# Batch 0 of an attention and MLP kernel: k and q of three head pairs loaded as bf16 by GpSimd's queue, fills moved to VectorE, and the front in another order

## The chip, the cores and the metric

The kernel runs on one core of one Trainium2 chip. The core has five engines, each with its own instruction queue: TensorE (PE in the profile, with its weight loads as PEld), VectorE (DVE), ScalarE (ACT), GpSimd (POOL) and SyncE (SP). The metric is the time of one execution on the device, in microseconds; lower is better.

## The reference

Four batches of chunked attention with 8 memory rows, and behind it an MLP with a snake activation. Cut to what matters:

```python
B, H, S, D = 4, 8, 768, 64;  chunk, left_ctx, right_ctx = 32, 16, 8;  n_mem = 8
for c in range(S // chunk):                       # 24 chunks
    q_c    = q[:, :, 32*c : 32*c + 32]
    k_full = concat(mem_k, k[:, :, max(0, 32*c - 16) : min(S, 32*c + 40)])
    v_full = concat(mem_v, v[:, :, same rows])
    a      = softmax(q_c @ k_full.T / 8)
    out[:, :, 32*c : 32*c + 32] = a @ v_full
x = out.transpose(0, 2, 1, 3).reshape(3072, 512)
h = x @ w_in                                      # 512 -> 2048
g = h + sin(alpha * h)**2 / (alpha + 1e-9)
result = g @ w_out                                # 2048 -> 512, float32
```

## The kernel before

Matmuls run in bf16 with sums in f32. A batch has 768 rows; its attention gives xT (features on the partitions, rows along them), and a dense stage per batch computes h = xT times w_in in 16 tiles of 128 features (`half_tile`, L458, 4 matmuls for each half of the rows), the sine on ACT (L473), the square (`squared`), the sum into gT on VectorE (L485) and the matmul with w_out (L496). The attention of batch b + 1 runs inside the dense stage of batch b. Only batch 0 has nothing to hide in: its attention is the *front*, `Stage(-1)`, and the dense stage of batch 0 begins when its xT is there.

The order of all work is written out by hand, as strings of words; each word calls one method of `Stage`, and every engine takes its instructions in the order in which the words issue them. Words that matter here, for head pair 0 to 3:

- `k0`, `l0`: `turn`, which transposes k or q of a pair on PE into a PSUM bank (L279 for batch 0, L285 for the other batches); `K0A`, `L0V`: `put_k` and `put_q`, which copy the result into kT and qT (L296 and L310) on ACT (A) or VectorE (V). `put_k` also copies the two ends, always on VectorE (L302).
- `a0A`, `a4V`: the cast of k (0 to 3) or q (4 to 7) of a pair from f32 to bf16 (L689).
- `s01`: scores of pair 0, half 1: the mask (L328), eight score matmuls (L336) and one exponential on ACT into pt (L343). `n0`: row sums by matmuls with ones (L358). `y0`, `r0`: on ACT, the logarithm of the sums (L367) and the exponential of its negative (L372), which gives 1/sum. `v01`: values of a pair and half (L378) and their product with 1/sum into xT (L383, VectorE).
- `z1`: one matmul of 512 columns on a tile of zeros into a bank that is not in use (L723); nothing reads its result.
- `V002`: loads v of heads 0 and 1 of batch 0; `I02`, `U69`: load column blocks of w_in and row blocks of w_out; `dq108`: loads q of batch 1, all heads, as bf16 (`load_one`, L155). All of these are DMAs of GpSimd's queue, which can convert f32 to bf16 on the way. `m0` copies the memory values into the v tile (L188).
- `Cb`, `Ci` and so on: constants. `Cb` and `Cm` make the score mask, `Ci` a table of it for `mind` (L799 to L805), `Cf` an f32 identity (L822), `Ck` the transposed memory keys (L811), `Cw` the bf16 memory values (L825), `Cl` alpha, `Cz`, `Cv`, `Cp` and `Cs` fill the borders of kT, the ones beside v, the ends of pt and the borders of kst.

k and q of batch 0 are loaded as f32 by SyncE's queue, eight loads of two heads each, and cast on chip. In the f32 tile the two heads lie one after the other; the cast interleaves them (`beside`), so that one transpose of 128 columns turns both heads at once: six per pair. The other batches load bf16 straight, and `turn` then needs one transpose per head: twelve of 64 columns.

Of the kernel before, what the change touches and what calls it, by code (L numbers as in the profile page):

```python
# [9 lines left out]
P = 128  # L10
# [5 lines left out]
F32 = mybir.dt.float32  # L16
ACTF = mybir.ActivationFunctionType
ALU = mybir.AluOpType
# [67 lines left out]
def kernel(  # L86
# [12 lines left out]
    nc = tc.nc  # L99
    B, H, S, D = q.shape  # L100
# [3 lines left out]
    NJ = S // QW  # L104
    HP = H // 2
# [9 lines left out]
    mlp = ctx.enter_context(tc.tile_pool(name="mlp", bufs=4))  # L115
# [7 lines left out]
    ident = consts.tile([P, P], BF, name="ident")  # L123
# [3 lines left out]
    asum = consts.tile([P, 8], BF, name="asum")  # L127
    mind = consts.tile([P, NJ, 3, 32], BF, name="mind")
# [12 lines left out]
    q_bf = consts.tile([P, H, 6, D], BF, name="q_bf")  # L141
# [124 lines left out]

    def beside(src, hp):

        return src[:, 2 * hp:2 * hp + 2].rearrange("p h r d -> p (h r d)").rearrange(
            "p (r h d) -> p r h d", r=6, h=2)

    def turn(b, src, hp):
        bank, bs = banks.single()
        t = bank[:, 0:384].bitcast(BF).rearrange("p (r c) -> p r c", r=6)
        if b == 0:
            for r in range(6):
                nc.tensor.transpose(  # L279
                    t[:, r, :], beside(src, hp)[:, r].rearrange("p h d -> p (h d)"), ident[:]  # L280
                )
            return t, bs
        for r in range(6):
            for e in range(2):
                nc.tensor.transpose(  # L285
                    t[64 * e:64 * e + 64, r, :], src[:, 2 * hp + e, r, :], ident[:]
                )
        return t, bs
# [248 lines left out]
    class Stage:  # L537
# [81 lines left out]
        def do_k(self, a):  # L619
            self.piece["k" + a] = turn(self.b, k_bf, int(a))  # L620

        def do_l(self, a):
            self.piece["q" + a] = turn(self.b, q_bf, int(a))
# [62 lines left out]
        def do_a(self, a):  # L686
            hp = int(a[0]) % HP
            dst = kq[int(a[0]) // HP]
            copier(a[1])(  # L689
                beside(dst, hp).rearrange("p r h d -> p h r d"),  # L690
                kq_f[int(a[0])][:].rearrange("p h (r d) -> p h r d", d=D),
            )
# [44 lines left out]

    kq_f = [mlp.tile([P, 2, 6 * D], F32, name="kq_f", tag=t) for t in ("u", "s2") * 4]  # L740
    memk_f = mlp.tile([P, H, D], F32, name="memk_f", tag="o_sb", bufs=3)
    alpha_rows = mlp.tile([FT, P], F32, name="alpha_rows", tag="o_sb", bufs=3)
    memv_f = mlp.tile([P, H, D], F32, name="memv_f", tag="o_sb", bufs=3)
# [1 line left out]
    def load_f(src, hp, t):  # L745
        nc.sync.dma_start(
            t[:], src[0, 2 * hp:2 * hp + 2].rearrange("h (p r) d -> p h (r d)", p=P)
        )

    nc.vector.memset(zeros[:], 0.0)  # L750
    nc.vector.memset(tiny[:], 0.0)
    load_f(k, 0, kq_f[0])
    load_f(q, 0, kq_f[4])
    for bb in range(B):
        if not CROSSED[bb][0]:
            nc.scalar.dma_start(memk_f[NM * bb:NM * bb + NM], mem_k[bb].rearrange("h n d -> n h d"))
    nc.scalar.dma_start(memv_f[64:72], mem_v[0].rearrange("h n d -> n h d"))
    nc.scalar.preload_act_table_set("natural_log_exp_and_others")
    for hp in (1, 2, 3):
        load_f(k, hp, kq_f[hp])  # L760
        load_f(q, hp, kq_f[4 + hp])
    nc.sync.dma_start(alpha_rows[:], moe_alpha.rearrange("(ft p) -> ft p", p=P))
    nc.vector.memset(ones[:], 1.0)
    nc.vector.memset(mcol[:], 0.0)
    masks.make_identity(nc, ident[:])
    for vw in vws:
        nc.gpsimd.memset(vw[0:32, 0, 0, 0:D], 0.0)
        nc.gpsimd.memset(vw[96:128, H - 1, NJ - 1, 0:D], 0.0)

    rows = ((0, 0, 56), (1, 32, 96), (2, 64, 128), (3, 16, 56), (4, 64, 120), (5, 64, 72))  # L770

# [23 lines left out]
        nc.vector.tensor_copy(mrow[:], mt)  # L795
        banks.give(bs)

    def const_i():
        nc.gpsimd.tensor_tensor(out=asum[:, 0:5], in0=ident[:, 0:5], in1=ident[:, 64:69], op=ALU.add)  # L799
        nc.gpsimd.tensor_tensor(out=asum[:, 5:7], in0=asum[:, 0:3:2], in1=asum[:, 3:5], op=ALU.add)  # L800
        nc.gpsimd.tensor_copy(
            mind[:], asum[:, 0:3].unsqueeze(1).unsqueeze(3).to_broadcast([P, NJ, 3, 32])
        )
        nc.gpsimd.tensor_copy(mind[:, 0, 0, :], asum[:, 5:6].to_broadcast([P, 32]))
        nc.gpsimd.tensor_copy(mind[:, NJ - 1, 2, :], asum[:, 6:7].to_broadcast([P, 32]))  # L805

    def const_k():
        bank, bs = banks.single()
# [23 lines left out]
        nc.vector.reciprocal(inv_alpha[:], alpha_sb[:])  # L832
        banks.give(bs)

    def const_z():
        for kT in kTs:
            nc.gpsimd.memset(kT[:, :, 0:16], 0.0)
            nc.gpsimd.memset(kT[:, :, 848:856], 0.0)

    def const_p():  # L840
        for pt in pts:
# [6 lines left out]
    def const_s():  # L848
        nc.gpsimd.memset(kst[0:32, 0, :], 0.0)
        nc.gpsimd.memset(kst[96:128, NJ - 1, :], 0.0)  # L850

    consts_of = dict(b=const_b, m=const_m, i=const_i, k=const_k, l=const_l, p=const_p, v=const_v,
                     s=const_s, z=const_z, f=const_f, w=const_w)

    first = {}
    stage = Stage(-1, None)
    stage.tile = first
    stage.run((
# [4 lines left out]
    ))  # L863
    for i, words in enumerate(((
# [54 lines left out]
```

## Time and profile before

| | us |
|---|---|
| median of 3 runs | 215.26 (214.52 to 215.56) |
| the profiled execution | 213.6 |
| its span, first to last instruction | 211.8 |
| busy in the span: PE, PEld | 201.2, 111.8 |
| busy in the span: DVE, ACT, POOL | 139.4, 144.8, 100.2 |
| dense matmuls of batch 0 unbroken from | 23.38 |

Times in the rows count from the start of the span. An engine's busy time is the union of its instructions; a matmul's row is longer than its share of PE, since matmuls are pipelined. A row of the time order has the start, the duration, the engine, the line of the kernel, the operation and the tiles; "x6" says that six equal instructions in a row are merged; what stands in brackets is the idle time of the engine ahead of it and what ended it. The chain of waits is followed back from the last instruction to whatever released each one. The landing of a load is when its semaphore tells that all data is there.

### The profile page before, as it was taken

How to read it: one execution, taken by the hardware profiler on the slowest of the kernel's cores; microseconds unless marked ns; L12 is line 12 of the kernel's file. 1: busy time of each engine (PE TensorE's matmuls, PEld its weight loads, DVE VectorE, ACT ScalarE, POOL GpSimd, SP SyncE). 2: the span in 40 equal slices, each digit the busy share in tenths (PEclk: the TensorE clock that was granted, in tenths of full speed). 3: DMA queues.
4: the chain of work that ended last, by engine and by line, in shares of the span. 5: the costliest groups of instructions: out<-in, count | busy, mean ns of one | idle time of the engine just before them, and what ended most of it. 6: DMA issues, size and time to landing. Idle time of an engine off the chain costs nothing.

```text
span 211.8 us, 4339 instructions
## 1 busy us (share of the span) xinstructions
PE 201.2 (95%) x1654; PEld 111.8 (53%) x1654; DVE 139.4 (66%) x211; ACT 144.8 (68%) x229; POOL 100.2 (47%) x140
## 2 busy tenths in 40 slices
PE   2978999999999999999999999999999999999993
PEld 1545565655455555554456555554555455554442
DVE  5896698998453669958585569895446287864011
ACT  4789898958837579969817398968764299991110
POOL 8997609496596490029981068589200022200000
DMA  6999999999999899949999339959744400000312
GB/s 204 321 195 161 208 207 204 205 156 176 180 158 106 163 145 130 165 99 112 142 224 128 102 57 150 181 87 143 150 117 108 136 0 3 0 2 14 137 50 99
DMA packets 95852, 28.20 MB, mean 133 GB/s; under 512 B 84808, under 2 KB 92376, under 8 KB 95832
## 3 DMA queue, kind: packets, MB, share of 16 engines
q0 software_dynamic: 68608, 13.25, 87.5%
q1 hardware_dynamic: 27008, 14.63, 27.9%
q8 instruction: 13, 0.21, 0.5%
q14 instruction: 7, 0.06, 0.1%
q10 hardware_dynamic: 216, 0.05, 0.1%
HBM read 29.66 MB, written 6.29 MB: 170 GB/s over the span
## 4 chain that ended last, share of the span: by engine, by line
PE 75%; DVE 12%; DMA 4%; issue 3%; ACT 3%; SPq 1%; POOL 1%; DVEq 0%
PE ps L496 35%; PE ps L458 32%; DMA kq_f<-in_k_dram 3%; PE ps L448 3%; DVE gT L485 2%; PE ps L419 2%; DVE s L481 2%; DVE qT L310 2%; DVE kT L296 2%; ACT u L473 1%; ACT s L478 1%; DMA xT<-x_blk 1%; DVE k_bf L689 1%; PE ps L405 1%; POOL s L481 1%
## 5 line engine op out<-in xcount | busy, mean ns | idle before, releaser
L496 PE MATMUL ps<-w_out_sb,gT 128*128 128x512 bf16 (+2 forms) x400 | 89.1, 371 | 0.0
L458 PE MATMUL ps<-xT,w_in_sb 128*128 128x384 bf16 x512 | 86.2, 326 | 1.1 <-DVE gT L485 0.4
L485 DVE SCALAR_TENSOR_TENSOR gT<-s,inv_alpha,ps 128x768 bf16<-128x768 f32 x64 | 63.1, 1012 | 12.3 <-ACT s L478 5.3
L458 PEld LDWEIGHTS <-w_in_sb 128*128 128x128 bf16 x512 | 49.7, 98 | 36.2 <-issue 3.0
L473 ACT ACTIVATE u<-ps,alpha_sb 128x768 f32<-128x768 f32 x64 | 56.6, 895 | 17.5 <-PE ps L458 15.0
L496 PEld LDWEIGHTS <-gT 128*128 128x128 bf16 x400 | 36.5, 98 | 37.9 <-DVE gT L485 0.2
L481 POOL TENSOR_TENSOR s<-u 128x768 f32<-128x768 f32 x11 | 17.2, 1568 | 67.1 <-ACT u L473 66.9
L433 ACT ACTIVATE pt<-ps,biasm 128x256 bf16<-128x256 f32 x72 | 27.2, 490 | 10.5 <-PE ps L419 10.5
L503 DVE COPY o_sb<-ps 128x512 f32<-128x512 f32 (+1 forms) x15 | 10.1, 678 | 28.3 <-PE ps L496 26.4
L481 DVE TENSOR_TENSOR s<-u 128x768 f32<-128x768 f32 x23 | 21.9, 953 | 7.8 <-ACT u L473 7.7
L478 ACT ACTIVATE s<-u 128x768 f32<-128x768 f32 x30 | 25.0, 841 | 0.5
L503 ACT COPY o_sb<-ps 128x512 f32<-128x512 f32 (+1 forms) x10 | 5.6, 562 | 21.6 <-PE ps L496 21.6
L393 DVE TENSOR_TENSOR x_blk<-ps,rinv 96x512 bf16<-96x512 f32 x24 | 16.5, 686 | 0.8
L179 POOL DMA_DIRECT2D vw<-in_v_dram x13 | 13.8, 1061 | 0.6 <-issue 0.6
L172 POOL DMA_DIRECT2D vw<-in_v_dram x13 | 11.8, 906 | 4.9 <-PE ps L405 4.9
L238 POOL DMA_DIRECT2D kst<-in_k_dram x16 | 12.7, 794 | 2.0 <-DMA vw<-in_v_dram 1.3
L392 DVE RECIPROCAL rinv<-ps 96x8 f32<-96x8 f32 x24 | 4.8, 198 | 12.5 <-PE ps L448 11.3
L232 POOL DMA_DIRECT2D kst<-in_k_dram x16 | 10.9, 682 | 3.4 <-DMA vw<-in_v_dram 2.8
L245 POOL DMA_DIRECT2D q_bf<-in_q_dram x12 | 10.7, 911 | 0.0
L448 PEld LDWEIGHTS <-pt 128*128 128x128 bf16 x192 | 8.2, 97 | 4.2 <-ACT pt L433 0.3
L448 PE MATMUL ps<-vw,pt 128*128 128x65 bf16 x192 | 8.9, 193 | 0.0
L408 ACT COPY xT<-ps 128x384 bf16<-128x384 bf16 x6 | 3.1, 509 | 7.7 <-PE ps L405 7.7
(91 smaller groups left out, 139.2 us busy)
## 6 DMA issues: line engine op xcount, KB each, us to landing
out_dram<-o_sb SPq DMA_DIRECT2D x23, 256.0 KB, 2.3
kq_f<-in_k_dram SPq DMA_DIRECT2D x4, 384.0 KB, 6.0
kq_f<-in_q_dram SPq DMA_DIRECT2D x4, 384.0 KB, 5.8
q_bf<-in_q_dram POOLq DMA_DIRECT2D x12, 128.0 KB, 6.5
w_in_sb<-in_moe_w_in_dram POOLq DMA_DIRECT2D x1, 1152.0 KB, 13.3
vw<-in_v_dram POOLq DMA_DIRECT2D x8, 112.0 KB, 7.5
vw<-in_v_dram POOLq DMA_DIRECT2D x7, 128.0 KB, 7.4
kst<-in_k_dram POOLq DMA_DIRECT2D x14, 64.0 KB, 4.8
```

The costliest lines, as they stand in the source:

```text
L179: nc.gpsimd.dma_start(vw[72:128, c0:hi, 0:D], win(vflat, base + QW * c0 + 48, hi - c0, 56))
L238: nc.gpsimd.dma_start(kst[72:72 + n, j, :].rearrange("p (h d) -> p h d", d=D), k[b, :, QW * j + 48:QW * j + 48 + n, :].rearrange("h p d -> ...
L393: nc.vector.tensor_tensor(out=x_blk[:].rearrange("p g e d -> p e g d"), in0=otv[0:QW, :, :, 0:D], in1=rinv[:].unsqueeze(3).to_broadcast([Q ...
L433: nc.scalar.activation(pt[:, 0:H * QW].rearrange("p (g e c) -> p g e c", g=2, e=4)[:, :, :, 32 * m:32 * m + 32], sc[:, :, 0:4 * QW].rearra ...
L448: nc.tensor.matmul(otv[:, e, hp, :], pt[:, QW * i:QW * i + P], vws[b % 2][:, 2 * hp + e, j, 0:D + 1],)
L458: nc.tensor.matmul(t["hT"][:, hf, 0:HALF], w_in_sb[:, kt, P * t["ft"]:P * t["ft"] + P], t["xT"][:, kt, HALF * hf:HALF * hf + HALF], start= ...
L473: nc.scalar.activation(t["u"][:], t["hT"][:, :, 0:HALF], ACTF.Sin, scale=alpha_sb[:, ft:ft + 1])
L478: nc.scalar.activation(s2[:], u[:], ACTF.Square)
L481: e.tensor_tensor(out=s2[:], in0=u[:], in1=u[:], op=ALU.mult)
L485: nc.vector.scalar_tensor_tensor(out=gT[:, ft, :].rearrange("p (e c) -> p e c", e=2), in0=t["s2"][:], scalar=inv_alpha[:, ft:ft + 1], in1= ...
L496: nc.tensor.matmul(o[:, c0:c1], gT[:, ft, P * s:P * s + P], w_out_sb[:, ft, c0:c1], start=(ft == 0), stop=(ft == FT - 1),)
L503: copier(state["engines"][state["o"] % len(state["engines"])])(o_sb[:, c0:c1], o[:, c0:c1])
```

## The change

Only pair 0 of batch 0 keeps the f32 load, the cast and the six whole transposes (`HARD`). k and q of pairs 1 to 3 are loaded as bf16 by GpSimd's queue (`dk024` and its like: k, batch 0, heads 2 to 3) and turned head by head, twelve transposes, as in the other batches; their six casts go. The fills of ident, of the v borders (L767, L768), of the kT borders and the table of `Ci` move from GpSimd to VectorE; the f32 identity moves from ACT to VectorE, the cast of the memory values from VectorE to ACT. The order of the front is written anew: 21 zero matmuls where there were 8, and `Cs`, which fills kst for batch 2, comes last.

```diff
+    HARD = ((0, False), (0, True))
...
     def turn(b, src, hp):
...
-        if b == 0:
+        if b == 0 and (hp, src is q_bf) in HARD:
             for r in range(6):
...
-    kq_f = [mlp.tile([P, 2, 6 * D], F32, name="kq_f", tag=t) for t in ("u", "s2") * 4]
+    kq_f = [None] * 8
+    for hp, isq in HARD:
+        kq_f[hp + HP * isq] = mlp.tile([P, 2, 6 * D], F32, name="kq_f", tag="u" if isq else "s2")
...
+    nc.vector.memset(ident[:], 0.0)
     nc.vector.memset(zeros[:], 0.0)
     nc.vector.memset(tiny[:], 0.0)
-    load_f(k, 0, kq_f[0])
-    load_f(q, 0, kq_f[4])
+    for hp, isq in HARD:
+        load_f(q if isq else k, hp, kq_f[hp + HP * isq])
...
-    for hp in (1, 2, 3):
-        load_f(k, hp, kq_f[hp])
-        load_f(q, hp, kq_f[4 + hp])
...
-    masks.make_identity(nc, ident[:])
+    masks.make_identity(nc, ident[:], nomemset=True)
     for vw in vws:
-        nc.gpsimd.memset(vw[0:32, 0, 0, 0:D], 0.0)
-        nc.gpsimd.memset(vw[96:128, H - 1, NJ - 1, 0:D], 0.0)
+        nc.vector.memset(vw[0:32, 0, 0, 0:D], 0.0)
+        nc.vector.memset(vw[96:128, H - 1, NJ - 1, 0:D], 0.0)
...
-    def const_i():
+    def const_i(eng="P"):
+        e = nc.gpsimd if eng == "P" else nc.vector
...
-    def const_z():
+    def const_z(eng="P"):
+        e = nc.gpsimd if eng == "P" else nc.vector
...
-        'Cb z1 Cz CfA Ci a0A V002 Ck Cs Cm k0 a4V K0A a1V V024 CwV Cp z1 l0 z1 L0A m0 a5A s01 k1 '
+        'z1 z1 Cb z1 dk024 CfV z1 dq024 CiV z1 CwA z1 dk046 dk068 Ck Cv Cm dq046 a4V z1 z1 a0A z1 '
+        'z1 k0 l0 k1 CzV K0V l1 L0A L1V K1A s01 dq068 V002 m0 V024 s00 s10 k2 V046 K2V n0 l2 y0 '
...
```

ACT up to its fourth exponential, before (memk_f and memv_f are the f32 memory rows, kT_85 and qT_87 the turned k and q of batch 0, pt_97 to pt_100 the exponentials of the scores, r_sb logarithm and reciprocal of the sums):

```order
L822 CAST ident_f<-ident 16x16
L689 CAST k_bf<-kq_f 128x2x6x64
L296 COPY kT_85<-ps 128x7x96
L310 COPY qT_87<-ps 128x768
L689 CAST q_bf<-kq_f 128x2x6x64
L343 ACTIVATE pt_97<-ps 128x768
L296 COPY kT_85<-ps 128x7x96
L343 ACTIVATE pt_98<-ps 128x768
L343 ACTIVATE pt_99<-ps 128x768
L367 ACTIVATE r_sb<-ps 128x768
L343 ACTIVATE pt_100<-ps 128x768
```

and after, where line 691 is the cast of before's line 689, 298 its 296, 312 its 310, 345 its 343, 369 its 367 and 374 its 372:

```order
L828 CAST memv_st<-memv_f 8x512
L691 CAST k_bf<-kq_f 128x2x6x64
L312 COPY qT_87<-ps 128x768
L298 COPY kT_85<-ps 128x7x96
L345 ACTIVATE pt_97<-ps 128x768
L345 ACTIVATE pt_98<-ps 128x768
L345 ACTIVATE pt_99<-ps 128x768
L369 ACTIVATE r_sb<-ps 128x768
L374 ACTIVATE r_sb<-r_sb 128x768
L345 ACTIVATE pt_100<-ps 128x768
```

The cast of the memory values now stands first; the k copy of pair 0 and the q cast of pair 1 are gone, and the k copy of pair 1 stands ahead of the first exponential instead of behind it.

GpSimd from the end of the identity to v of heads 0 and 1, before:

```order
masks.py:199 AFFINE_SELECT ident<-ident 128x128
L767 MEMSET vw_89 32x64
L837 MEMSET kT_85 128x4x16
L799 TENSOR_TENSOR asum<-ident 128x5
L800 TENSOR_TENSOR asum<-asum 128x2
L801 COPY mind<-asum 128x768
L168 DMA vw_89<-in_v_dram 48x64
L172 DMA vw_89<-in_v_dram 64x15x64
L179 DMA vw_89<-in_v_dram 56x16x64
```

and after, where line 155 is the bf16 load:

```order
masks.py:199 AFFINE_SELECT ident<-ident 128x128
L155 DMA k_bf<-in_k_dram 128x2x384
L155 DMA q_bf<-in_q_dram 128x2x384
L155 DMA k_bf<-in_k_dram 128x2x384 x2
L850 MEMSET vw_89 128x64
L850 MEMSET vw_90 128x64
L155 DMA q_bf<-in_q_dram 128x2x384 x2
L168 DMA vw_89<-in_v_dram 48x64
L172 DMA vw_89<-in_v_dram 64x15x64
L179 DMA vw_89<-in_v_dram 56x16x64
```

(In the first of the two, five fills like those shown and two small copies into mind are left out.) Six loads and the ones beside v stand ahead of v where the fills and the table stood; before, that last fill stood behind the first w_in load.

PE from the mask's transpose (L794, after: L796) to the q turn of pair 0, before; each pair of rows of a turn stands for six:

```order
L794 MATMUL ps<-ident,mcol 128x128
L279 LDWEIGHTS k_bf
L279 MATMUL ps<-ident,k_bf 128x128
L723 LDWEIGHTS zeros
L723 MATMUL ps<-zeros 128x512
L279 LDWEIGHTS q_bf
L279 MATMUL ps<-ident,q_bf 128x128
```

and after, up to the k turn of pair 1 by heads (L287); the zero matmul (L725) stands four times ahead of the k turn:

```order
L796 MATMUL ps<-ident,mcol 128x128
L725 LDWEIGHTS zeros
L725 MATMUL ps<-zeros 128x512
L281 LDWEIGHTS k_bf
L281 MATMUL ps<-ident,k_bf 128x128
L281 LDWEIGHTS q_bf
L281 MATMUL ps<-ident,q_bf 128x128
L287 LDWEIGHTS k_bf
L287 MATMUL ps<-ident,k_bf 64x128
```

Behind the rows shown follow, before, a zero matmul and the first scores; after, the q turn of pair 1 by heads and then the first scores. Six zero matmuls, where one stood, come ahead of the memory keys' transpose, which comes just ahead of the mask's.

More of the change, by code (lines that the diff above doesn't have):

```diff
@@ L796, in const_m @@
         banks.give(bs)
-    def const_i():
-        nc.gpsimd.tensor_tensor(out=asum[:, 0:5], in0=ident[:, 0:5], in1=ident[:, 64:69], op=ALU.add)
-        nc.gpsimd.tensor_tensor(out=asum[:, 5:7], in0=asum[:, 0:3:2], in1=asum[:, 3:5], op=ALU.add)
-        nc.gpsimd.tensor_copy(
+    def const_i(eng="P"):
+        e = nc.gpsimd if eng == "P" else nc.vector
+        e.tensor_tensor(out=asum[:, 0:5], in0=ident[:, 0:5], in1=ident[:, 64:69], op=ALU.add)
+        e.tensor_tensor(out=asum[:, 5:7], in0=asum[:, 0:3:2], in1=asum[:, 3:5], op=ALU.add)
+        e.tensor_copy(
             mind[:], asum[:, 0:3].unsqueeze(1).unsqueeze(3).to_broadcast([P, NJ, 3, 32])
         )
-        nc.gpsimd.tensor_copy(mind[:, 0, 0, :], asum[:, 5:6].to_broadcast([P, 32]))
-        nc.gpsimd.tensor_copy(mind[:, NJ - 1, 2, :], asum[:, 6:7].to_broadcast([P, 32]))
+        e.tensor_copy(mind[:, 0, 0, :], asum[:, 5:6].to_broadcast([P, 32]))
+        e.tensor_copy(mind[:, NJ - 1, 2, :], asum[:, 6:7].to_broadcast([P, 32]))
     def const_k():
@@ L833, in const_l @@
         banks.give(bs)
-    def const_z():
+    def const_z(eng="P"):
+        e = nc.gpsimd if eng == "P" else nc.vector
         for kT in kTs:
-            nc.gpsimd.memset(kT[:, :, 0:16], 0.0)
-            nc.gpsimd.memset(kT[:, :, 848:856], 0.0)
+            e.memset(kT[:, :, 0:16], 0.0)
+            e.memset(kT[:, :, 848:856], 0.0)
     def const_p():
```

5 rows, old and new, of the table stage are left out of this document.

## The prediction

> **What bounds the kernel now.** I read the stretches of time first, then the chain of waits, then the front engine by engine. A row of the stretches gives the busy time of PE, PEld, DVE, ACT and POOL:
>
> ```profile
> 8.89:22.53 13.64, 11.57 (x193) 7.08 (x191) 11.66 (x21) 12.67 (x18) 12.35 (x24) 1.00 2.15 201
> 23.38:208.58 185.20, 184.14 (x1429) 101.73 (x1428) 121.17 (x164) 126.43 (x206) 79.21 (x91) 1.00 1.12 123
> ```
>
> From 23.38 to 208.58 PE idles 1.1 of 185.2 us. So the end is the start of the dense matmuls (L458) plus an almost unbroken stretch, and this change, which lies ahead of 23.38, moves the time only by moving that start, unless a later load comes too late. What sets the start stands in the chain of waits (start, us, work):
>
> ```profile
> 7.16 0.64 DVE k_bf L689
> 11.24 0.95 DVE k_bf L689
> 13.85 0.55 DVE k_bf L689
> 15.27 0.71 DVE q_bf L689
> 22.78 0.56 DVE xT L383
> ```
>
> and in the time order of PE and ACT (start, us, engine, line; in brackets the idle time ahead and what ended it):
>
> ```profile
> 23.38 8.94 PE L458 MATMUL ps<-xT,w_in_sb 128*128 128x384 bf16 x54 [0.26 <-DVE xT L383]
> 4.02 0.83 ACT L689 CAST k_bf<-kq_f 128x768 bf16<-128x768 f32 x1 [0.50 <-DMA kq_f<-in_k_dram]
> 8.89 0.81 ACT L343 ACTIVATE pt<-ps 128x768 bf16<-128x768 f32 x1
> 11.65 0.81 ACT L343 ACTIVATE pt<-ps 128x768 bf16<-128x768 f32 x1 [0.64 <-PE ps L336]
> 15.70 1.51 ACT L343 ACTIVATE pt<-ps 128x768 bf16<-128x768 f32 x2 [0.23 <-PE ps L336]
> 20.86 0.80 ACT L367 ACTIVATE r_sb<-ps 128x768 f32<-128x768 f32 x1
> 21.69 0.84 ACT L372 ACTIVATE r_sb<-r_sb 128x768 f32<-128x768 f32 x1
> ```
>
> Read alone, the chain blames VectorE and its casts (L689). But ACT, from its first exponential (8.89) to the end of its last reciprocal of a row sum (21.69 + 0.84 = 22.53), is busy 12.67 of 13.64 us, with 8 exponentials (L343), 4 logarithms (L367), 4 exponentials of those (L372) and copies. The last piece of x that the fourth dense matmul needs (L383, 22.78 to 23.34) waits for that last ACT result. So two engines are nearly full, and work taken from one brings little unless the other starts sooner or loses work too.
>
> **The price of each part.** The rows of PE and ACT on which it rests:
>
> ```profile
> 4.59 0.57 PE L811 MATMUL ps<-ident_f,memk_f 16*128 16x16 f32 x4 [2.79 <-DMA memk_f<-in_mem_k_dram]
> 5.17 0.85 PE L279 MATMUL ps<-ident,k_bf 128*128 128x128 bf16 x6
> 5.81 0.63 PE L723 MATMUL ps<-zeros 128*128 128x512 bf16 x1
> 9.17 0.50 PE L279 MATMUL ps<-ident,q_bf 128*128 128x128 bf16 x6
> 9.60 0.34 PE L328 MATMUL ps<-mind,mrow 64*128 64x384 bf16 x2
> 41.31 0.53 PE L285 MATMUL ps<-ident,k_bf 128*64 128x128 bf16 x12
> 10.19 0.83 ACT L343 ACTIVATE pt<-ps 128x768 bf16<-128x768 f32 x1
> ```
>
> those of VectorE:
>
> ```profile
> 5.20 0.23 DVE L815 CAST memkT<-ps 128x64 bf16<-128x64 f32 x1 [1.59 <-PE ps L811]
> 5.87 0.55 DVE L689 CAST q_bf<-kq_f 128x768 bf16<-128x768 f32 x1
> 7.83 0.71 DVE L825 CAST memv_st<-memv_f 8x512 bf16<-8x512 f32 x1
> 8.57 1.48 DVE L188 COPY vw<-memv_st 8x4096 bf16<-8x4096 bf16 x1
> 12.78 0.86 DVE L296 COPY kT<-ps 128x672 bf16<-128x672 bf16 x1
> 13.68 0.26 DVE L302 COPY kT<-ps 128x96 bf16<-128x96 bf16 x1
> 14.31 0.95 DVE L310 COPY qT<-ps 128x768 bf16<-128x768 bf16 x1
> ```
>
> those of GpSimd, four by time and three groups of its first 24 us (busy us, mean ns of one):
>
> ```profile
> 1.02 0.29 POOL masks.py:199 TENSOR_SCALAR_AFFINE_SELECT ident<-ident 128x128 bf16<-128x128 bf16 x1
> 14.81 0.78 POOL L213 DMA_DIRECT2D w_in_sb<-in_moe_w_in_dram  x1
> 20.98 0.89 POOL L155 DMA_DIRECT2D q_bf<-in_q_dram  x1 [0.84 <-PE ps L378]
> 21.86 0.88 POOL L155 DMA_DIRECT2D k_bf<-in_k_dram  x1
> L179 POOL DMA_DIRECT2D vw<-in_v_dram x4 | 4.9, 1236 | 0.0
> L172 POOL DMA_DIRECT2D vw<-in_v_dram x4 | 3.3, 837 | 0.0
> L846 POOL MEMSET vw<- 128x64 bf16 x2 | 1.0, 827 | 0.0
> ```
>
> and of its loads from issue to landing (the last row: all of v in the first 45 us):
>
> ```profile
> q_bf<-in_q_dram POOLq DMA_DIRECT2D x1, 768.0 KB, 16.4
> k_bf<-in_k_dram POOLq DMA_DIRECT2D x1, 768.0 KB, 19.3
> w_in_sb<-in_moe_w_in_dram POOLq DMA_DIRECT2D x1, 256.0 KB, 7.1
> vw<-in_v_dram POOLq DMA_DIRECT2D x1, 64.0 KB, 2.5
> DMA to landing us min/median/max: 6.2/7.7/10.8
> ```
>
> *PE to the first score.* The k turn of pair 0 began at 5.17. Now six zero matmuls come first (PE idled 2.79 us there, so they cost nothing; without that idle time, 6 x 0.43 = 2.6), and four more stand between the mask's transpose and that turn. Six transposes, 768 columns, took from 5.17 to 5.81, 0.64 us; 512 columns take 0.43 at this pace, and four times that is 1.7: the k turn starts at 5.17 + 1.7 = 6.9. ACT gives the same. Its cast of the memory values (0.71) now stands ahead of its cast of k, and their load was issued on ACT's queue right behind the one that PE awaited until 4.59. No row shows its landing; the bounds are 4.6 and 7.83, where the cast ran without a wait. I take 5.2, nearest to the load just ahead of it, and k is cast by 5.2 + 0.71 + 0.83 = 6.75.
>
> Then come, still ahead of the first scores, the q turn of pair 0 and both turns of pair 1 by heads. Twelve head transposes take 0.53 against 0.50 for six whole ones: twice the instructions, no time. At the slow pace three turns end their issue at 6.9 + 3 x 0.65 = 8.85, the fourth, at the pace of 9.17, near 9.4. From 9.60 the scores needed until 10.19, 0.6, to start an exponential: it starts at 10.0 instead of 8.89, **+1.1**. The k copy of pair 0, moved from ACT to VectorE (0.86 + 0.26), and its q copy on ACT (0.80) are done by 8.9 and 9.2, in time.
>
> *ACT from there.* The k copy of pair 1 now comes ahead of the first exponential, so 16 instructions are left of 17. Two in a row take 1.51, each alone 0.81: one follows another after 0.70, elsewhere up to 0.77, and a dependent one after 0.83 (20.86 to 21.69). 13 x 0.73 + 2 x 0.83 + 0.84 = 12.0, against 13.64 now. The waits of 0.64 and 0.23 go, as VectorE is ahead. Late next is the q copy of pair 2: after the q turn of pair 1 (9.6) VectorE has 0.95 + 0.26 + 1.48 + 0.86 + 0.26 + 0.95 = 4.8, some 4.6 as neighbours overlap; these scores reach ACT at 14.7, where it would be free at 14.5: +0.2. The series ends at 10.0 + 12.2 = 22.2; 12.2 - 13.64 = **-1.4**.
>
> *Behind it.* From 22.53 to 23.38 there are 0.85 us; VectorE was held until 22.78 by its previous piece, and about 0.75 stays: **-0.1**.
>
> *VectorE.* Five casts of k and q (the four of the chain, 2.85, and one of 0.54) and that of the memory values (0.71) go, the k copy of pair 0 comes. The fills and the mask table that it takes over fall into its 1.59 us of idle time ahead of 5.20 and cost nothing; if they overran, the q cast, done at 6.42, has until 7.55.
>
> *The loads.* SyncE issues six fewer, which nobody awaits. GpSimd issues six at 0.88 each from 1.3 on: q of pair 1 at 2.2. The two 768 KB loads landed at 37.4 and 41.2, so a pair's 192 KB takes 3.8 / 4 = 0.95 in a busy queue; behind pair 0 (in by 5.87) q of pair 1 lands at 7.8 and is needed at 8.85. No cost, with 1 us to spare; bounds 2.5 and 10.8 us after issue, 4.7 and 13.0. Each later pair is wanted over 1 us after landing. In GpSimd's queue the six loads (5.3) and the fill of vw (1.0) now stand ahead of v (4.9 + 3.3, and at most 0.8 for its small first load) and w_in, so w_in is issued at 1.3 + 15.3 = 16.6 and lands between 19.1 (2.5) and 23.7 (7.1, as now, 14.81 to 21.9). I take 20, near the short end, because six f32 loads on SyncE's queue no longer share the DMA engines with v. It is needed at 22.1. The later loads keep their order behind it, so they come earlier by as much as PE does.
>
> **Sum.** 1.1 - 1.4 - 0.1 = -0.4. The profiled execution took 213.6 and the runs' median is 215.26, 1.7 more; from the median, 214.8. Its own range is -0.9 (memory values at 4.6, fast pace a little sooner) to +0.9 (w_in at 23.7, the fourth matmul 0.5 later): 214.3 to 216.1. Under 0.5% (1.08 us) no change can be told from noise.
>
> **Rivals.** *PE reaches its fast pace earlier.* A turn took 0.64 at 5.17 and 0.3 less at 9.17, 4.6 us after PE's steady work began; the ten zero matmuls start at 1.2. If they bring the fast pace by 6.9, three turns save 0.3 each, the exponentials start 0.95 sooner, at 9.05, and the time is 213.9; with the memory values in at 4.6, 213.3. Against it: PE still idles from 3.8 to 4.6. The Trainium skill, "TensorE: Matmul & The Clock Gate", Part 1, says that the clock opens after a busy window of about 3.4 us, and that the windows run free of the kernel's start; by it this rival is right if a window with that gap in it counts as busy. The trace agrees with such a delay (4.6 us), and shows nothing on how full a window must be.
>
> *GpSimd's queue is slow at first (the slower side).* Place: the q turn of pair 1, ahead of all scores in PE's order. Landing 10.8 after issue, as a load of v did, it is there at 13.0, the first exponential starts at 14.0 and all shifts by 4.0: 218.8. With the median of 7.7: 9.9, 10.9 and 215.7. It decides for slower from a landing at 10.5 on. For it: v's loads all needed at least 6.2. Against it: they stood behind eight f32 loads, now it is two.
>
> *VectorE alone was the bound,* as the chain says: its four cast pieces, 2.85 us, go, 212.4. Against: ACT's 16 instructions need 12 us behind an exponential that waits for a k cast at 6.75 and four turns.
>
> **Chances.** Forecast 0.42, early pace 0.38, slow queue 0.15, VectorE 0.05. Faster by over 0.5%: three quarters of the early pace, the last, and a little of the forecast, 0.37; within: 0.48; slower: most of the slow queue and a little of the forecast, 0.15. The range 213.2 to 216.2 holds the forecast, nearly all of the early pace, and the slow queue up to its median.
>
> **What would show it.** The first exponential near 10.0 (9.0 for the early pace, after 11 for the slow queue); ACT without a wait over 0.3 us from there to the last reciprocal near 22.2; the dense matmuls unbroken from 22.9; zero matmuls of 0.63 until about 7; no wait of PE for k or q of pairs 1 to 3; w_in in ahead of 22. It is wrong if PE waits at the head turns, if a new wait enters ACT's series, or if the stretch behind the start is no longer unbroken.

## The result, and the profile after

The changed kernel takes 213.28 us (median of 20 executions, 212.64 to 214.35), the kernel before in the same job 215.29 (20 executions, 213.43 to 216.77): a ratio of 0.9926, 95% interval 0.9901 to 0.995 (the ratio is estimated from all executions; that of the two medians would be 0.9907). The two profiled executions are much closer: 213.12 after (span 211.3), 213.6 before (span 211.8). So there are two things to explain: 0.5 us between the profiles, and 2.0 us between the medians.

The same stretches of the changed kernel (busy time of PE, PEld, DVE, ACT and POOL, then granted clock, DMA share and GB/s):

```profile
8.89:22.53 13.64, 12.83 (x233) 7.49 (x230) 10.09 (x18) 12.84 (x18) 12.93 (x24) 1.00 2.35 168
23.38:208.58 185.20, 182.34 (x1409) 101.32 (x1425) 120.72 (x163) 126.19 (x205) 79.24 (x91) 1.00 1.11 123
```

VectorE went from 11.66 to 10.09 us in the first stretch; ACT is as full as before. PE's idle time in the long stretch seems to have grown, but 20 matmul records fewer are in the second row, so its busy time can't be compared that closely.

PE and ACT of the changed kernel in time order:

```profile
1.28 2.74 PE L725 MATMUL ps<-zeros 128*128 128x512 bf16 x6 [1.28 <-DVE zeros L755]
4.91 1.03 PE L725 MATMUL ps<-zeros 128*128 128x512 bf16 x4
6.91 0.51 PE L281 MATMUL ps<-ident,k_bf 128*128 128x128 bf16 x6 [0.98 <-ACT k_bf L691]
8.66 0.53 PE L287 MATMUL ps<-ident,q_bf 128*64 128x128 bf16 x12 [0.43 <-DMA q_bf<-in_q_dram]
22.83 3.47 PE L460 MATMUL ps<-xT,w_in_sb 128*128 128x384 bf16 x20 [0.15 <-DVE xT L385]
5.39 0.61 ACT L828 CAST memv_st<-memv_f 8x512 bf16<-8x512 f32 x1 [2.06 <-DMA memv_f<-in_mem_v_dram]
6.03 0.83 ACT L691 CAST k_bf<-kq_f 128x768 bf16<-128x768 f32 x1
9.67 2.21 ACT L345 ACTIVATE pt<-ps 128x768 bf16<-128x768 f32 x3 [0.45 <-PE ps L338]
21.17 0.84 ACT L374 ACTIVATE r_sb<-r_sb 128x768 f32<-128x768 f32 x1
```

The first exponential starts at 9.67 (before: 8.89). From there to the end of the last reciprocal, 21.17 + 0.84 = 22.01, ACT needs 12.34 us (before: 13.64), and the fourth dense matmul starts at 22.83 (before: 23.38). The front ends 0.55 us sooner. None of that reaches the end as it is. At the turn of batch 1's k, which had no wait before, PE now waits for the load:

```profile
39.73 1.29 PE L287 MATMUL ps<-ident,q_bf 128*64 128x128 bf16 x36
41.39 0.53 PE L287 MATMUL ps<-ident,k_bf 128*64 128x128 bf16 x12 [0.37 <-DMA k_bf<-in_k_dram]
```

Matched matmul by matmul, the changed kernel is 0.48 us ahead from 25 to 38.8, 0.11 ahead behind this wait, and level (0.04 behind) from 73 to 166. Then before loses 0.45 us at the last turned xT of batch 3, which SyncE transposes by DMA; 0.29 of it stands as idle time in the profile of before, and the changed kernel has no such wait there:

```profile
167.09 2.11 PE L458 MATMUL ps<-xT,w_in_sb 128*128 128x384 bf16 x12 [0.29 <-DMA xT<-x_blk]
```

So the 0.5 us of the pair is not the front's gain, though it is almost equal to it. One execution of each kernel is too little here.

### The profile page after: what moved, and what is told of

Its sections match the earlier page's. It is cut to its first block, busy times and chain, and to the rows that moved or that the text cites. A ratio compares the mean times of both kernels' runs of the same rounds, so it can differ in the third digit from the quotient of the medians.

```text
span 211.3 us, 4407 instructions
## 1 busy us (share of the span) xinstructions
PE 201.6 (95%) x1683; PEld 111.9 (53%) x1703; DVE 138.4 (66%) x221; ACT 143.7 (68%) x227; POOL 100.7 (48%) x132
## 4 chain that ended last, share of the span: by engine, by line
PE 75%; DMA 7%; ACT 6%; DVE 6%; issue 3%; POOL 2%; DVEq 0%
PE ps L498 37%; PE ps L460 31%; DMA w_out_sb<-in_moe_w_out_dram 4%; DMA q_bf<-in_q_dram 3%; PE ps L450 3%; PE ps L421 2%; DVE gT L487 2%; ACT s L480 2%; ACT u L475 1%; ACT pt L345 1%; ACT r_sb L369 1%; PE ps L407 1%; DVE qT L312 1%; DVE s L483 1%; POOL s L483 1%
## 5 line engine op out<-in xcount | busy, mean ns | idle before, releaser
L498 PE MATMUL ps<-w_out_sb,gT 128*128 128x512 bf16 (+2 forms) x382 | 87.1, 370 | 1.4 <-issue 0.3
L435 ACT ACTIVATE pt<-ps,biasm 128x256 bf16<-128x256 f32 x72 | 27.2, 490 | 10.5 <-PE ps L421 10.5
L505 DVE COPY o_sb<-ps 128x512 f32<-128x512 f32 (+1 forms) x15 | 10.1, 678 | 28.4 <-PE ps L498 23.7
L172 POOL DMA_DIRECT2D vw<-in_v_dram x13 | 12.3, 945 | 4.9 <-PE ps L407 4.7
L179 POOL DMA_DIRECT2D vw<-in_v_dram x13 | 12.3, 947 | 0.9 <-DMA q_bf<-in_q_dram 0.4
L245 POOL DMA_DIRECT2D q_bf<-in_q_dram x12 | 10.7, 911 | 0.0
L725 PE MATMUL ps<-zeros 128*128 128x512 bf16 x19 | 6.9, 462 | 1.4 <-DVE zeros L755 1.3
## 6 DMA issues: line engine op xcount, KB each, us to landing
w_in_sb<-in_moe_w_in_dram POOLq DMA_DIRECT2D x1, 1152.0 KB, 12.2
w_out_sb<-in_moe_w_out_dram POOLq DMA_DIRECT2D x2, 384.0 KB, 10.7
```

The lines of the kernel that those rows point to most:

```text
L172: nc.gpsimd.dma_start(vw[0:64, lo:c1, 0:D], win(vflat, a, n, 64))
L179: nc.gpsimd.dma_start(vw[72:128, c0:hi, 0:D], win(vflat, base + QW * c0 + 48, hi - c0, 56))
L435: nc.scalar.activation(pt[:, 0:H * QW].rearrange("p (g e c) -> p g e c", g=2, e=4)[:, :, :, 32 * m:32 * m + 32], sc[:, :, 0:4 * QW].rearra ...
L498: nc.tensor.matmul(o[:, c0:c1], gT[:, ft, P * s:P * s + P], w_out_sb[:, ft, c0:c1], start=(ft == 0), stop=(ft == FT - 1),)
L505: copier(state["engines"][state["o"] % len(state["engines"])])(o_sb[:, c0:c1], o[:, c0:c1])
```

## The experiments

They ran in three jobs, the first two on one chip, the third on another, and each took its own runs of the kernel before: e1 to e4 with 214.75 (median of 27 executions), e5 to e8 with 214.48 (29), e9 to e12 with 215.07 (23). Ratios are against the job's own runs.

**e1: the ten zero matmuls of the front taken out of the changed kernel.**

```diff
-        'z1 z1 Cb z1 dk024 CfV z1 dq024 CiV z1 CwA z1 dk046 dk068 Ck Cv Cm dq046 a4V z1 z1 a0A z1 '
-        'z1 k0 l0 k1 CzV K0V ...
+        'z1 Cb dk024 CfV dq024 CiV CwA dk046 dk068 Ck Cv Cm dq046 a4V a0A '
+        'k0 l0 k1 CzV K0V ...
```

> The changed kernel without its ten zero matmuls ahead of the first turn; the other eleven stay. Theory A (the gain is work taken off VectorE and ACT): PE turns at the slow pace, three turns of 0.65 behind the k cast at 6.9, first exponential near 10.2 instead of 9.67, about +0.5 us on the changed kernel, 213.7. Theory B (the gain is that PE's clock opens early in every run, where it opened at another time in each run of before): turns of 0.85 and 0.65 until 8 to 11, first exponential 10 to 11, +1.0 to +1.5 us, 214.3 to 214.8, and single times spread over 3 us as those of before do, not over 1.7.

213.33 (212.78 to 215.84), ratio 0.9928 [0.9901, 0.9956]: like the changed kernel with its zeros, and below what either theory said. The ten zero matmuls give nothing to the median. They don't bring the early pace reliably either: of three profiles with them (see e11 and e7) one has it. In the profile of e1 all four turns ran at the slow pace and the first exponential came at 10.62. That execution was its slowest, and shows where 2 us can go late in the kernel. GpSimd's first v load of batch 3, in time order:

```profile
140.22 1.29 POOL L172 DMA_DIRECT2D vw<-in_v_dram  x1
```

the chain of waits there (start, us, work), with the last of SyncE's turning transfers of q:

```profile
140.62 6.21 DMA qT<-q_bf
...
146.97 0.34 PE ps L421 x8
```

and, among the waits around qT, how long PE sat idle for that transfer (us, times):

```profile
  DMA qT<-q_bf: 2.0, 1
```

In the profile of before, SyncE issued it at 139.5 and the v load followed at 140.1, and it landed 2.4 us after issue; here the v load was 0.40 us ahead, and it took 6.2. I call this a photo finish: which of the two queues issues first is decided by a few tenths of a us.

**e2: six zero matmuls added to the front of before.**

```diff
-        'Cb z1 Cz CfA Ci ...
+        'Cb z1 z1 z1 z1 z1 z1 Cz CfA Ci ...
```

> The kernel before with six more zero matmuls ahead of the memory keys' transpose, where PE idles, and nothing else. Theory A: nothing to 0.3 us, 215.0 to 215.3, since VectorE's casts set the pace. Theory B: the clock opens by 5 us in every run, the q turn and its copy come 0.3 to 0.7 sooner, first exponential near 8.3, median 213.8 to 214.4, and the single times come closer together, within 2 us.

214.75, ratio 0.999 [0.9956, 1.0025]: nothing, as e1 from the other side. In its profile the k turn ran at the fast pace, yet the first exponential came at 9.76 instead of 8.89, because q of pair 1 landed at 9.00:

```profile
4.88 0.51 PE L279 MATMUL ps<-ident,k_bf 128*128 128x128 bf16 x6
9.03 0.83 ACT L689 CAST q_bf<-kq_f 128x768 bf16<-128x768 f32 x1 [1.32 <-DMA kq_f<-in_q_dram]
9.76 0.80 ACT L343 ACTIVATE pt<-ps 128x768 bf16<-128x768 f32 x1
```

ACT's series still ended at 22.69, only 0.16 later than in the first profile of before. So a late landing needn't reach the end of the series; here w_in, which landed at 23.16, held the first dense matmul until 23.21 (22.47 there).

**e3: the changed kernel with pairs 1 to 3 loaded as f32 by SyncE and cast; order, fills and zeros kept, save for the casts and the q turn of pair 1.**

```diff
-    HARD = ((0, False), (0, True))
+    HARD = tuple((hp, isq) for hp in range(4) for isq in (False, True))
...
-        'z1 k0 l0 k1 CzV K0V l1 L0A L1V K1A s01 dq068 ...
+        'z1 k0 l0 a1V k1 CzV K0V L0A a5A l1 L1V K1A s01 ...
```

> The changed kernel with k and q of pairs 1 to 3 loaded as f32 by SyncE and cast on VectorE (one on ACT) and turned whole, as before; fills, order and zero matmuls as changed. Theory A: five casts, 3.5 us, return to VectorE and one to ACT: the copies of pairs 2 and 3 are late, first exponential near 10, second half of the series waits 1 to 2 us, 214.3 to 215.3. Theory B: the early clock stays and most of the gain with it, 213.3 to 213.8.

221.55, ratio 1.030 [1.0261, 1.034]. ACT's waits from 9 to 32 us:

```profile
ACT pt L345 <- PE ps L338: 5.5, 5, 2.9
ACT r_sb L369 <- PE ps L360: 2.1, 1, 2.1
ACT q_bf L691 <- DMA kq_f<-in_q_dram: 0.7, 1, 0.7
```

Both theories fell far short. PE's granted clock read 0.50 from 12 to 24 in this profile, and its turns took 0.82 us there, but executions with a mean clock of 0.997 to 1.0 took 220.92 to 222.16 as well. Without the bf16 loads the new order is a loss; it takes for granted that no cast stands between a load and its turn.

**e4: the changed kernel with fills and mask table on GpSimd again, ahead of its loads.** 
```diff
-    nc.vector.memset(ident[:], 0.0)
-    masks.make_identity(nc, ident[:], nomemset=True)
+    masks.make_identity(nc, ident[:])
...
-        nc.vector.memset(vw[0:32, 0, 0, 0:D], 0.0)
+        nc.gpsimd.memset(vw[0:32, 0, 0, 0:D], 0.0)
...
-        'z1 z1 Cb z1 dk024 CfV z1 dq024 CiV z1 CwA ...
+        'z1 z1 Cb z1 Cz CfV z1 Ci dk024 dq024 z1 CwA ...
```

> The changed kernel with the identity's fill, the v and kT borders and the mask table on GpSimd again, ahead of its first load. GpSimd starts its loads 2.6 us later (3.95 instead of 1.43). Both theories, if the landing follows the issue: q of pair 1 lands near 10.5 to 11.2 instead of 8.62, first exponential 11.5 to 12.2, 214.8 to 215.8. If the landing is set by the two f32 loads and by the DMA engines, not by the issue, it lands near 9 and the time stays within 0.4 us, 213.3 to 213.7.

215.17, ratio 1.0016 [0.9988, 1.0045]: the whole gain is lost, 1.9 us. GpSimd's first load, PE's q turn of pair 2, and ACT's fourth and fifth exponential:

```profile
3.97 0.94 POOL L155 DMA_DIRECT2D k_bf<-in_k_dram  x1
13.06 0.53 PE L287 MATMUL ps<-ident,q_bf 128*64 128x128 bf16 x12 [1.19 <-DMA q_bf<-in_q_dram]
14.07 0.81 ACT L345 ACTIVATE pt<-ps 128x768 bf16<-128x768 f32 x1 [0.47 <-PE ps L338]
15.38 0.81 ACT L345 ACTIVATE pt<-ps 128x768 bf16<-128x768 f32 x1 [0.50 <-PE ps L338]
```

The first load is issued at 3.97 instead of 1.43. The first exponential still starts at 9.80; but k of pair 2 lands at 10.5 instead of 9.6 and q at 13.0 instead of 11.6, two waits of half a microsecond enter the series, and it ends at 23.13. So for pair 1 the second case held (q of pair 1, issued 2.5 us later, landed at 8.75 instead of 8.62), for pair 2 the first. The series accounts for 1.1 us. Some 0.6 more lie outside the span: in all twelve executions the time is 2.2 to 2.5 us longer than the span, against 1.7 to 1.9 in every other kernel here, and no trace shows why. By the spans alone e4 (median 212.7) stays 0.3 us ahead of before (213.0) and 1.1 behind e1 (211.6).

**e8: before, with that part alone: fills and table by VectorE, GpSimd's first v load at 1.72 instead of 3.95.** 
```diff
+    nc.vector.memset(ident[:], 0.0)
-    masks.make_identity(nc, ident[:])
+    masks.make_identity(nc, ident[:], nomemset=True)
...
-        nc.gpsimd.memset(vw[0:32, 0, 0, 0:D], 0.0)
+        nc.vector.memset(vw[0:32, 0, 0, 0:D], 0.0)
...
-        nc.gpsimd.tensor_copy(
+        nc.vector.tensor_copy(
             mind[:], asum[:, 0:3].unsqueeze(1).unsqueeze(3).to_broadcast([P, NJ, 3, 32])
...
-            nc.gpsimd.memset(kT[:, :, 0:16], 0.0)
+            nc.vector.memset(kT[:, :, 0:16], 0.0)
```

> The kernel before with one part of the change alone: the fills and the mask table by VectorE, so that GpSimd's first v load is issued near 1.4 instead of 3.95; f32 loads, casts and order stay. Theory C, that the gain is GpSimd's loads starting 2.5 us sooner (with the fills back on GpSimd the changed kernel lost all of it): w_in lands 0.5 to 1 sooner, at 21 to 22, and the median falls by 0.8 to 1.5, to 213.5 to 214.2. Theory D, that it needs the bf16 loads: v started sooner takes the transfer engines from the f32 loads of k and q, pair 1 lands later than 8.1 and the first exponential comes after 9.0, so that the median is 214.8 or more.

214.98, ratio 1.002 [0.9984, 1.0056]: nothing, as theory D said. In its profile q of pair 1 landed at 8.88 and ACT's cast waited:

```profile
8.90 0.83 ACT L689 CAST q_bf<-kq_f 128x768 bf16<-128x768 f32 x1 [0.41 <-DMA kq_f<-in_q_dram]
9.64 0.80 ACT L343 ACTIVATE pt<-ps 128x768 bf16<-128x768 f32 x1
```

D's reason, that v takes the transfer engines from the f32 loads, isn't shown: in four executions with v started as before that load landed between 8.13 and 9.57 (below).

So these parts bring nothing or a loss (e3, order and fills without the loads: +3.0%; e8, the fills: +0.2%; e4, loads and order without the fills: +0.2%, or -0.1% by the spans), and the whole brings 0.74%. The bf16 loads in the old order were not run.

**e6 and e10: before, unchanged, profiled again. e11: the changed kernel again.** No edit.

> The kernel before, unchanged, profiled in one more execution. Theory A (the stall at 147): first dense matmul behind the front near 22.5, and where the time is over 215, a TensorE gap of some 2 us near 147. Theory B (the front varies): q of pair 1 lands near 9 instead of 8.1, w_in near 23 instead of 21.9, the dense start is 0.7 to 1 us behind that of the first profile, and the time is 214.2 or more without a gap at 147.

> The kernel before, unchanged, a third execution profiled. Counting from the front (ninth dense matmul of batch 0: 24.18 in the first profile, 26.86 in the second), all profiles of kernels with before's front so far fit front + 14.6 to 15.0 + 34.5 + 68.4 + 25.5 to 26.6 + 18.6 + 25.5 + 1.8. Theory L (the front sets it): ninth dense matmul at 24.5 to 25.5, and the time is within 0.7 of that sum taken with the smallest of each stretch. Theory T (the tail of the kernel sets it): ninth dense matmul at 24.2, time over 214.3, lost between 142 and 168.

> The changed kernel, unchanged, a second execution profiled. Theory L: its front varies less, the ninth dense matmul stands at 23.6 to 24.4 (23.64 in its first profile; 24.33 and 24.38 in two close relatives), and the time is 212.7 to 213.9 without a clock under 0.99. Theory T: the front as before's, the difference lies behind 142.

e6 took 215.87, e10 214.2, e11 213.21, and each fits the theory that puts the difference into the front (B and L) better than its rival: no TensorE gap near 147 in e6, the ninth dense matmul at 24.98 in e10 and 23.86 in e11. ACT's cast of q of pair 1 in time order, in the first profile of before (the exponential behind it, at 8.89, stands in the prediction):

```profile
8.15 0.83 ACT L689 CAST q_bf<-kq_f 128x768 bf16<-128x768 f32 x1
```

in e5 below, which has the same front, with the exponential:

```profile
8.70 0.83 ACT L689 CAST q_bf<-kq_f 128x768 bf16<-128x768 f32 x1 [0.67 <-DMA kq_f<-in_q_dram]
9.44 0.80 ACT L343 ACTIVATE pt<-ps 128x768 bf16<-128x768 f32 x1
```

in e10:

```profile
9.03 0.83 ACT L689 CAST q_bf<-kq_f 128x768 bf16<-128x768 f32 x1 [0.48 <-DMA kq_f<-in_q_dram]
9.77 0.80 ACT L343 ACTIVATE pt<-ps 128x768 bf16<-128x768 f32 x1
```

and in e6:

```profile
9.59 0.83 ACT L689 CAST q_bf<-kq_f 128x768 bf16<-128x768 f32 x1 [1.59 <-DMA kq_f<-in_q_dram]
10.33 0.80 ACT L343 ACTIVATE pt<-ps 128x768 bf16<-128x768 f32 x1
```

In before the cast stands ahead of the first exponential, so this starts 0.76 us after q of pair 1 lands, each time: landings at 8.13, 8.68, 9.01 and 9.57, exponentials at 8.89, 9.44, 9.77 and 10.33. The profile that I predicted from had the earliest of the four; there ACT's copy ahead of the cast ended at 8.14, so that a still earlier landing would have brought nothing. In e6 PE then stood 0.64, 0.79 and 0.89 us between 8.5 and 12.5, and its granted clock (the number behind POOL's) fell, where in the first profile it stayed at 1.00; three stretches of e6:

```profile
9.00:12.00 3.00, 1.62 (x24) 1.02 (x24) 2.90 (x4) 2.41 (x4) 2.96 (x11) 0.97 1.24 322
12.00:16.00 4.00, 3.52 (x36) 2.08 (x37) 3.19 (x7) 2.73 (x4) 2.30 (x3) 0.50 2.73 164
16.00:20.00 4.00, 3.82 (x42) 2.30 (x41) 3.80 (x8) 3.31 (x6) 3.46 (x7) 0.67 3.54 136
```

The front of the changed kernel in e11, in time order: the k and q turns of pair 1 and the first exponential.

```profile
8.23 0.83 PE L287 MATMUL ps<-ident,k_bf 128*64 128x128 bf16 x12
8.87 0.52 PE L287 MATMUL ps<-ident,q_bf 128*64 128x128 bf16 x12
9.87 2.21 ACT L345 ACTIVATE pt<-ps 128x768 bf16<-128x768 f32 x3
```

And in e7 below, which has the same front, the q turn of pair 1 and the first exponential:

```profile
9.09 0.85 PE L287 MATMUL ps<-ident,q_bf 128*64 128x128 bf16 x12
10.70 2.21 ACT L345 ACTIVATE pt<-ps 128x768 bf16<-128x768 f32 x3 [0.64 <-PE ps L338]
```

Here PE's pace moves the start, not a landing: the fast pace began near 4.5 in the first profile, 8.9 in e11, and 10.4 in e7. All seven profiles with an unaltered front:

| front | first exponential | ACT series | fourth dense matmul | time |
|---|---|---|---|---|
| before, first profile | 8.89 | 13.64 | 23.38 | 213.6 |
| before, e5 | 9.44 | 13.46 | 23.74 | 214.78 |
| before, e10 | 9.77 | 13.56 | 24.17 | 214.2 |
| before, e6 | 10.33 | 14.88 | 26.06 | 215.87 |
| after, first profile | 9.67 | 12.34 | 22.83 | 213.12 |
| after, e11 | 9.87 | 12.17 | 23.06 | 213.21 |
| after, e7 | 10.70 | 12.21 | 23.57 | 213.92 |

The dense start is at 24.34 on average before (23.76 without e6) and 23.15 after. It doesn't set the time alone: e5's comes 0.43 sooner than e10's and its time is 0.58 longer, as PE waits late in e5 for the last turned xT:

```profile
168.25 1.95 PE L458 MATMUL ps<-xT,w_in_sb 128*128 128x384 bf16 x11 [0.93 <-DMA xT<-x_blk]
```

That wait is 0.29 in the first profile of before, 0.25 in e11, and absent in e6, e10, e7 and the first profile of the changed kernel.

**e7: in the changed kernel, four dense matmuls ahead of the k turn that waits at 41.39.**

```diff
-... L0A L2A q13P k2 q11V Ube b15 U9b g11 ...
+... L0A L2A q13P q11V Ube b15 k2 U9b g11 ...
```

> The changed kernel, with the four matmuls of one dense group ahead of the turn of batch 1's k of pair 2 (they stand behind it in the changed kernel). There that turn waited for its load, which landed at 41.35 as in before (41.2), and the front's lead of 0.48 us over before shrank to 0.11 at this place. Theory F, that this landing is a floor that takes back what the front gains: TensorE's dense matmuls behind it run 0.3 to 0.4 earlier and the median falls to 212.9 to 213.1. Theory N, that something behind it (transfers of the next batch) sets the pace anyway: no change, 213.2 to 213.4.

213.39, ratio 0.994 [0.9909, 0.9971]: no change against the changed kernel. Theory F failed, but the test isn't clean: in the profile the moved matmuls wait instead for a PSUM bank that ACT is still emptying, and the k load landed at 40.79, sooner than in the other profile. Whether N's reason holds isn't shown.

```profile
42.15 0.81 PE L460 MATMUL ps<-xT,w_in_sb 128*128 128x384 bf16 x4 [0.45 <-ACT qT L312]
```

**e5: before, with two small fills (zeros written into zeros) ahead of GpSimd's last v load.** It should take the photo finish of e1 away.

```diff
-... q13P X3 V305 h12 ...
+... q13P X3 Cd V305 h12 ...
```

> The kernel before, with GpSimd filling a used-up tile twice (about 1.1 us) ahead of the last batch's first v load, which otherwise is issued at 140.1, 0.6 us behind SyncE's last turning transfer of q (139.5 in the profile of before; in the run without front zeros the v load came 0.4 ahead of it, that transfer landed 6.2 later and TensorE stood for 2.0 at 147). Theory A, that a lost photo finish there is what spreads the times of before over 3.3 us and puts its median 1.7 above its profiled execution: median near 213.7, spread under 2 us, no TensorE gap over 1 us near 147. Theory B, that the front is what varies (landings of the eight f32 loads and of w_in): median as before, 214.8 to 215.3, spread over 2.5 us.

214.85 (213.96 to 216.76), ratio 1.0024 [0.9986, 1.0063]. Theory A fell: the lost photo finish is real, but it isn't what sets before's median or its spread. (In its profile the v load came 1.77 us behind the last q transfer, and PE had no wait near 147. Whether the fills cost something later, in the wait at 168.25 above, is open.)

**e9: before, with two zero matmuls at each of the three places where PE stood in e6.**

```diff
-... L0A m0 a5A s01 k1 l1 L1V K1A s00 s10 ...
+... L0A m0 a5A s01 z2 k1 z2 l1 L1V K1A z2 s00 s10 ...
```

> The kernel before, with pairs of zero matmuls put where TensorE stood in the second profile of before: ahead of the turns of k and q of pair 1 and ahead of the first scores behind them. There it stood 0.64, 0.79 and 0.89 us between 8.5 and 12.5, the granted clock fell to 0.50 from 12 to 16 and to 0.67 from 16 to 20, and the dense start came 2.68 later than in the first profile, where the stalls were 0.99 in all and the clock stayed at 1.00. Theory G, that idle time in before's front lets the clock fall and that this is what the slow half of its executions pays: no execution with a granted clock under 0.99, the highest time under 215.8, median 213.8 to 214.2. Theory L, that the landings of the f32 loads vary and the clock only adds to the slowest few: a narrower upper end, but a median of 214.4 to 215.2, since zeros take up to 0.5 where nothing is late.

214.80 (213.66 to 216.49), ratio 1.0014 [0.9981, 1.0048]. The upper end (over 216 in 3 of 12) and the median stayed: theory G fell, and of L the median held, the narrower upper end not. No execution had a mean granted clock under 0.99, but in before only 4 of the 79 whose clock is recorded had, so twelve say little on that; the fallen clock can explain only a few of before's executions.

**e12: the changed kernel with the scores of pair 0 ahead of pair 1.**

```diff
-... z1 CwA z1 dk046 ... a0A z1 z1 k0 l0 k1 CzV K0V l1 L0A L1V K1A s01 dq068 V002 m0 V024 s00 s10 ...
+... z1 z1 dk046 ... a0A CwA z1 z1 k0 l0 CzV K0V L0A s01 k1 l1 s00 L1V K1V dq068 V002 m0 V024 s10 ...
```

> The changed kernel with the first scores ahead of pair 1: ScalarE casts k of pair 0 ahead of memv, TensorE takes both heads' scores of pair 0 ahead of and between the turns of pair 1, and VectorE instead of ScalarE copies k of pair 1. The first exponential then waits for no load of pair 1 (q landed at 8.62 in the profile of the changed kernel) and starts at 8.6 to 9.0 instead of 9.67. Theory S, that the ScalarE series from the first exponential sets the dense start: series ends near 21.2 instead of 22.0, dense start limited by w_in at 21.9, median 212.6 to 212.9. Theory F, that transfers landing at 41 (k of batch 1) take back what the front gains: 213.1 to 213.4 although the dense start is earlier. Theory V, that pair 1, now turned later and copied by VectorE, is late for the third exponential: no gain in the series, 213.2 to 213.8.

214.46, ratio 1.0003 [0.9967, 1.0039]: the gain is gone. ACT's first three exponentials, and PE at the scores of the third:

```profile
8.75 0.81 ACT L345 ACTIVATE pt<-ps 128x768 bf16<-128x768 f32 x1 [0.43 <-PE ps L338]
9.99 0.81 ACT L345 ACTIVATE pt<-ps 128x768 bf16<-128x768 f32 x1 [0.42 <-PE ps L338]
12.01 0.81 ACT L345 ACTIVATE pt<-ps 128x768 bf16<-128x768 f32 x1 [1.21 <-PE ps L338]
11.62 0.34 PE L338 MATMUL ps<-qT,kT 64*128 64x96 bf16 x8 [1.51 <-DVE kT L304]
```

Theory V: the series starts 0.92 sooner than in the changed kernel and ends 1.16 later, at 23.17, since all copies of pair 1 now queue on VectorE and the last is there at 11.57. Feeding ACT without a break is worth more than starting it early.

## Why the prediction was right or wrong

- *First exponential, +1.1 (at 10.0).* Right in kind. 9.67, 9.87 and 10.70 in three profiles; my case of three turns at the slow pace is what e11 shows (9.87). In the first profile the early-pace rival was right about PE, as the four zeros took 1.03 and the turn 0.51. It didn't reach 9.05, because the memory values came at 5.37 (I took 5.2), k was cast by 6.86 (6.75), and q of pair 1 landed at 8.62. That last term was mis-sized: I had 7.8, with 1 us to spare, and PE waited 0.43 us. The 0.6 from scores to exponential was misread: at 10.19 ACT came straight from its k copy (9.59 to 10.30), not from a wait for scores. That it was near the mark (0.55 in the first profile and e11) is luck.
- *ACT's series, -1.4 (12.2 us).* Right: 12.34, 12.17 and 12.21, a gain of 1.3 to 1.5 against the first profile. This is the change's lasting gain; the wait of 0.2 that I left at the scores of pair 2 shows as 0.09 and 0.17. "Each later pair is wanted over 1 us after landing" failed for q of pair 2, which landed at 11.60 and was turned at 11.64.
- *Behind it, -0.1.* 22.01 to 22.83 is 0.82, 0.03 less than before. Small, and too hopeful.
- *VectorE.* The fills overran: the q cast was done at 6.92 instead of 6.42. As I said, that cost nothing; PE's q turn came at 7.26.
- *The loads.* w_in landed at 21.85 against my 20, inside the bounds of 19.1 to 23.7, 0.2 us ahead of the first dense matmul. Two errors offset each other here. It was issued at 14.72, not 16.6, as GpSimd's queue took 13.3 us ahead of it instead of 15.3; and it landed 7.1 us after issue, as before, not 3.4. So the reason for the near end, that six f32 loads no longer share the transfer engines, has nothing for it; with the issue that I had, w_in would have come at 23.7, too late. "The later loads come earlier by as much as PE does" failed at batch 1's k: it landed at 41.35, 0.15 later than before, and took back 0.37 of the lead.
- *VectorE alone the bound; slow queue.* Both fell. VectorE has 1.6 us less to do in the stretch and ACT still sets the end; q of pair 1 landed 6.3 us after issue, near the 6.2 that I named as the least for v. The queue's issue didn't set that landing: issued at 4.90 in e4, it landed 3.9 later, at nearly the same time (8.75).
- *The sum.* -0.4 was forecast for the pair of profiles, -0.5 came, partly by luck (0.45 of it is lost by before at 166). The median, 213.28, lies inside 213.2 to 216.2, but 0.08 above its lower end, and outside the forecast's own 214.3 to 216.1. It lies at the early pace's 213.3, but not for that rival's reason: e11 had that time without an early pace, and so had e1's median without the zeros. That the range held is luck too. The step that failed is the one behind the sum: "from the median, 214.8" (215.26 - 0.4 is 214.86). It carried a difference worked out from one execution over to the median, as if the 1.7 us between the two lay outside the front. Its front was the earliest of four. In before's profiles the first exponential hangs on one f32 landing that comes between 8.13 and 9.57. The change took that cast out of ACT's way, and as a bf16 load q of pair 1 landed between 8.25 and 8.62 in three profiles. Against the typical start of before the first exponential is 0.5 later, not 1.1 (mean 10.08 against 9.61), and the gain of the series remains. So the dense start moves by -0.6 to -1.2, not -0.5, and the time by 2.0 us in the first job; against their own runs of before, e1 gains 1.4 and e7 1.1. The front's part of this is seen in seven profiles; no run changed that landing alone.

**What stays open.** Of 99 timed executions of before, 44 are over 215.1; of 43 with the changed front (changed kernel, e1, e7), one. Without these, the medians are 214.29 and 213.33, 1.0 apart, about what the dense starts give; but 215.1 is a limit that I chose, and it takes nearly half of one side away, so this is an agreement and no proof. Why before has so many over 215.1, I can't say; e6, with its fallen clock, is the only profile of one of them. The lost photo finish (e5) and stalls that let the clock fall (e9) were tested and don't explain it; e12, whose PE again waits in the front, has 5 of 12 there. A pace of PE that opens late, which the granted clock doesn't show, is not borne out by the profiles at hand: in those of before the k turn of pair 1 was fast at 8.52 in e5, and both turns were still slow until 10.7 in e10, which took less time (214.2 against 214.78).

## What to carry to other kernels

Before a difference is worked out from one profiled execution, its time is to be held against the median: where they differ by more than the change is worth, the waits for loads in that profile are the first suspects, and a second profile of the kernel before is worth more than a finer sum. A cast that stands in order ahead of the first work of the busiest engine passes every delay of its load on; a load that lands in the final type passes it on through PE alone (0.43 us in one of three profiles here). And parts of such a change needn't add up: loads, fills and order gave 0.74% together, and nothing or a loss in the three combinations that were run.

## What the runs showed of the hardware

- The same front reached PE's fast pace at about 4.5, 8.9 and 10.4 us in three executions, with the zero matmuls at the same times (1.28, and 4.90 to 5.22). The Trainium skill, "TensorE: Matmul & The Clock Gate", Part 1, says that the window which opens the clock is free-running and doesn't reset when a kernel starts. That the three differ agrees with it. Their spread of 5.9 us is more than the window of about 3.4 us that the prediction takes from the same place, so that its position at the start can't be all of it.
- The granted clock in the profile read 1.00 while 512 columns took 0.43 us (six zero matmuls in 2.74), twice what they took later (0.22, four in 1.03): the pace at the start must be read from durations. It did show the fall in e6, to 0.50, behind stalls of PE of which none was over 0.9 us; in e2 stalls of 0.27, 1.03 and 0.61 us between 8 and 12 were followed by 1.00.
- A turning transfer that landed 2.4 us after issue took 6.2 in e1, when a GpSimd load of v was issued 0.40 us ahead of it, and 3.9 in e9, where the load was 0.02 ahead; both are single executions.
